# Transposing all 128 rows of every token tile, the last one of an expert included

## The chip, the cores and the metric

The kernel runs on one core of a Trainium2 chip (trn2). The metric is the device time of one execution in microseconds (us). Six terms recur: PE is the matrix engine TensorE, PEld its weight loads (they are shown as a row of their own because they can run beside a matmul), ACT is ScalarE, DVE is VectorE, POOL is GpSimd, and SP issues most of the DMA transfers. PSUM is the memory that PE writes its results to, in banks of 512 float32 columns.

## The reference

Two stages are chained. The first is a gated linear attention over 4 batches, 8 heads, 768 steps and 48 dimensions per head. Its output, laid out as 3072 tokens of 384 numbers, goes through a mixture of 8 experts: every token goes to the one expert with its largest gate logit.

```python
for t in range(S):                                   # attention
    state = f[:, :, t, :, None] * state + np.einsum('bhd,bhe->bhde', k[:, :, t], v[:, :, t])
    y[:, :, t] = np.einsum('bhd,bhde->bhe', q[:, :, t], state)
...
for e in range(E):                                   # experts, x: 3072 x 384
    mask = e_idx == e
    h = np.maximum(x[mask] @ w1[e], 0.0)             # 384 -> 1024
    ye = h @ w2[e]                                   # 1024 -> 384
    out[mask] = gate_w[mask, None] * eom[mask, e, None] * ye
```

## The kernel before, in words

**Two stages.** Up to about 130 us of the span the kernel computes the attention in 24 chunks of 128 tokens, writes every finished token row into a slot of a DRAM table (`xs_dram`) that belongs to its expert, and starts on the first expert. From then on it runs the eight experts one after the other, sorted by their number of tokens, the largest first (`Experts.run`).

**The slots of an expert.** The expert at place s is given a fixed number of token columns, `CAPS = (512, 448, 432, 416, 400, 400, 384, 376)`. Its tokens come from DRAM as tiles of `TS` = 128 rows (`tokens_in`, line 655, always whole tiles of 128 rows; a slot without a token holds a row that was cleared in advance). `rows(s)` (line 641) cuts the capacity into tiles: 448 is 128 + 128 + 128 + 64, so the last tile of that expert counts 64 rows, and those of the following ones 48, 32, 16, 16, 128 (384 is three whole tiles) and 120. The expert at place 0 has four whole tiles.

**One expert.** For each expert PE computes `mm1` (line 750: eight groups of 9 matmuls, 384 to 1024, because each float32 operand is split into a high and a low part and three products are made) and then `mm2` (line 773, or `mm2_rows`, line 787, for experts with at most three tiles: 72 matmuls, 1024 to 384). A matmul of `mm1` or `mm2` streams as many columns as the expert has token columns, 512 down to 376, so it gets shorter from expert to expert. ACT and DVE take each group out of PSUM (lines 765 and 766) and split the weights of the next expert (`split`, line 630).

**The step that the change touches.** `mm1` needs the tokens with the 384 features on the partitions, while they come from DRAM with a token per partition. So `x_in(s, c)` (line 721) turns them, for each of the `KC` = 3 pieces c of 128 features: one PE transpose per tile into columns j*128 of one PSUM tile `x_ps`, then `x_split` (line 714) takes the capacity's columns out: ACT makes the high part `xh` (line 717), DVE the low part `xl` (line 718). A transpose is a weight load of the tile's piece followed by a matmul against the identity. `x_tr` (line 709) passes the tile's count n of rows: the transpose loads n rows, uses an n x n identity and writes n columns. The whole tiles and the short one of an expert follow each other directly, three or four transposes in a row; such a row of transposes is called a block here. There is one `x_ps` tile only (pool `psx`, one buffer), so a block waits until DVE has finished with the block before it.

**What sets the order.** Each engine executes its instructions in the order in which the program is written (`chain`, line 1054, fixes it for DVE, ACT, POOL and PE). In `run`, the three `x_in` blocks of expert s+1 and the weight splits for its `mm1` are spread over the eight steps of `mm2` of expert s: the list `front` (lines 891 to 896) holds them, and one entry is taken out after each step f (or after two of three steps in `mm2_rows`). So 21 blocks stand in the middle of `mm2` matmuls, three per expert from place 1 to 7. The transposes of the expert at place 0 stand elsewhere (`x_early`, `x_late`) and are of whole tiles. The way back, after `mm2`, is `put` (line 811): PE transposes the result tile by tile, ACT scales it, and POOL scatters the rows to the output.

Of the kernel before, what the change touches and what calls it, by code (L numbers as in the profile page):

```python
# [26 lines left out]
TS = 128  # L27
# [100 lines left out]
def attention(ctx, tc, nc, k, kpool, rt, q01, k01, f01, q23, k23, f23, v, wg, xs_dram, r, ex):  # L128
# [334 lines left out]
    for t in range(last + 1):  # L463
# [32 lines left out]
        if hot(t - 2):  # L496
            x_tr(t - 2)
# [52 lines left out]
    scatter(len(sq))  # L550
    evac_y(last)
    x_tr(last - 1)
    run_pq()
    evac_x(last - 1)
    ex.mm1_early(0)
    x_tr(last)
    evac_x(last)
    route(len(RG) - 1, last - 1, 2)
# [19 lines left out]
class Experts:  # L578
# [128 lines left out]
            self.gq.pop(0)()  # L707

    def x_tr(self, s, c, ps, j, col):
        t, n = self.xg[s, j]  # L710
        self.nc.tensor.transpose(out=ps[:, col:col + n], in_=t[0:n, c * 128:(c + 1) * 128],  # L711
                                 identity=self.k.ident[0:n, 0:n])

    def x_split(self, pool, c, ps, n, width, name):
        hi = pool.tile([128, width], F32R, name=f"{name}h{c}")
# [417 lines left out]
```

## Time and profile before

| what | value |
|---|---|
| time, median of 3 runs | 380.4 us (378.98 to 382.08) |
| the profiled execution's own time | 383.17 us |
| its span | 381.4 us |
| mean granted clock of PE | 0.998 of full speed |
| busy in the span: PE, PEld, DVE, ACT, POOL | 95%, 88%, 62%, 52%, 38% |
| DMA: bytes moved, mean rate | 67.75 MB, 178 GB/s |

The span is the time from the first to the last instruction that the profiler saw; the execution's own time has 1.8 us around it. The times of the profile below count from the span's start. A busy PE is not a PE at its peak, because matmuls are pipelined and each is shown from its start to the end of its pipeline; what PE really delivers is read from the distance between the starts of neighbouring matmuls.

### The profile page before, as it was taken

Reading aid. Unit: us, or ns where it says so; the run is one execution under the profiler, and the core shown is the slowest. Engines: PE = TensorE matmul, PEld = TensorE weight load, DVE = VectorE, ACT = ScalarE, POOL = GpSimd, SP = SyncE. Lnnn points to the kernel's source line nnn. Section 1 sums busy time; section 2 is a strip of 40 time slices with the busy share of each in tenths; the row PEclk is TensorE's granted clock in tenths of the full one; section 3 lists DMA queues with packets and bytes.
Section 4 is the critical chain, followed back from the end, with each engine's and each line's share of the span. In section 5 each row is a group of like instructions: output and inputs, shape, how many; then the busy total and the mean of one; then the engine's idle time right before and its main releaser. Section 6 shows DMA issues by size and latency. Waiting matters only on the chain. (4 is left out here: it accounts for less than half of the span.)

```text
span 381.4 us, 8425 instructions
## 1 busy us (share of the span) xinstructions
PE 363.3 (95%) x3199; PEld 334.6 (88%) x3199; DVE 234.7 (62%) x482; ACT 197.7 (52%) x468; POOL 145.8 (38%) x176
## 2 busy tenths in 40 slices
PE   7899999998979999999999999999999999999993
PEld 2688978897868899989989999999999999999993
DVE  6988979897994773655644545463554554554610
ACT  3576856865745641536525634543652653753510
POOL 6686787997968670002201210310220220233012
PEclk9999999999999999999999999999999999999999
DMA  8999999999139327853434353445354354331001
GB/s 262 350 358 358 310 245 247 290 274 281 47 108 306 137 93 235 306 170 123 148 99 171 137 171 128 158 158 169 125 188 147 125 177 157 124 101 42 16 23 41
DMA packets 49315, 67.75 MB, mean 178 GB/s; under 512 B 3682, under 2 KB 43893, under 8 KB 49264
## 3 DMA queue, kind: packets, MB, share of 16 engines
q1 hardware_dynamic: 45952, 57.46, 49.6%
q0 software_dynamic: 3312, 9.65, 7.0%
q8 instruction: 27, 0.44, 0.5%
q14 instruction: 24, 0.20, 0.2%
HBM read 54.16 MB, written 13.39 MB: 177 GB/s over the span
## 5 line engine op out<-in xcount | busy, mean ns | idle before, releaser
L822 POOL DMA_INDIRECT out<-o,dst x30 | 30.2, 1007 | 188.3 <-ACT o L817 102.6
L766 DVE SCALAR_TENSOR_TENSOR hl<-h_ps,hh 128x256 fp32r<-128x256 f32 (+6 forms) x72 | 39.3, 546 | 53.1 <-ACT hh L765 52.3
L761 PE MATMUL h_ps<-xh,w1h 128*128 128x400 f32 (+6 forms) x192 | 67.3, 351 | 0.3 <-DVE hl L766 0.3
L761 PE MATMUL h_ps<-xh,w1l 128*128 128x400 f32 (+6 forms) x192 | 65.0, 338 | 0.0
L761 PE MATMUL h_ps<-xl,w1h 128*128 128x400 f32 (+6 forms) x192 | 64.9, 338 | 0.0
L765 ACT ACTIVATE hh<-h_ps 128x256 fp32r<-128x256 f32 (+6 forms) x72 | 34.8, 484 | 50.3 <-PE h_ps L761 48.6
L783 PE MATMUL y_ps<-hh,w2h 128*128 128x256 f32 (+4 forms) x168 | 57.7, 343 | 0.0
L783 PE MATMUL y_ps<-hl,w2h 128*128 128x256 f32 (+4 forms) x168 | 55.7, 332 | 0.0
L783 PE MATMUL y_ps<-hh,w2l 128*128 128x256 f32 (+4 forms) x168 | 55.6, 331 | 0.0
L718 DVE TENSOR_TENSOR xl<-x_ps,xh 128x400 fp32r<-128x400 f32 (+6 forms) x23 | 13.1, 568 | 41.8 <-ACT xh L717 38.5
L761 PEld LDWEIGHTS h_ps<-xh,w1h 128*128 128x128 f32 x192 | 36.1, 188 | 1.2 <-DVE hl L766 0.5
L761 PEld LDWEIGHTS h_ps<-xl,w1h 128*128 128x128 f32 x192 | 36.2, 188 | 0.4
L761 PEld LDWEIGHTS h_ps<-xh,w1l 128*128 128x128 f32 x192 | 36.0, 188 | 0.5
L717 ACT CAST xh<-x_ps 128x400 fp32r<-128x400 f32 (+6 forms) x23 | 11.3, 490 | 48.5 <-PE x_ps L711 42.4
L224 POOL TENSOR_TENSOR q_t<-q_t,p 128x512 f32<-128x512 f32 x24 | 30.6, 1276 | 9.6 <-DVE p L210 8.0
L637 DVE TENSOR_TENSOR w2l<-w2r,w2h 128x768 fp32r<-128x768 f32 x31 | 30.7, 991 | 4.2 <-ACT w2h L636 1.3
L783 PEld LDWEIGHTS y_ps<-hh,w2h 128*128 128x128 f32 x168 | 31.6, 188 | 1.0
L783 PEld LDWEIGHTS y_ps<-hl,w2h 128*128 128x128 f32 x168 | 31.6, 188 | 0.5
L783 PEld LDWEIGHTS y_ps<-hh,w2l 128*128 128x128 f32 x168 | 31.7, 188 | 0.4
L246 PE MATMUL a_ps<-q_t,k_t 64*128 64x128 f32 x384 | 28.3, 285 | 3.3 <-DVE k_t L221 2.7
L210 DVE TENSOR_TENSOR_SCAN p<-f_ps,start_p 128x511 f32<-128x511 f32 x22 | 28.0, 1273 | 3.9 <-ACT start_p L198 2.2
L323 PE MATMUL x_ps<-turn,xt 128*128 128x112 f32 x192 | 26.2, 280 | 3.8 <-ACT xt L317 3.6
(175 smaller groups left out, 773.1 us busy)
## 6 DMA issues: line engine op xcount, KB each, us to landing
w1r<-in_w SPq DMA_DIRECT2D x32, 384.0 KB
w2r<-in_w SPq DMA_DIRECT2D x32, 384.0 KB
xg<-xs_dram SPq DMA_DIRECT2D x5, 802.0 KB
xs_dram<-empty SPq DMA_DIRECT2D x8, 401.0 KB
f_t<-in_f SPq DMA_DIRECT2D x6, 512.0 KB
q_t<-in_q SPq DMA_DIRECT2D x6, 512.0 KB
k_t<-in_k SPq DMA_DIRECT2D x6, 512.0 KB
v_t<-in_v SPq DMA_DIRECT2D x6, 512.0 KB
```

The costliest lines, as they stand in the source:

```text
L210: nc.vector.tensor_tensor_scan(out=flat(d["p"])[:, 1:n], data0=flat(d["f"])[:, 0:n - 1], data1=sp[:, 1:n], initial=sp[:, 0:1], op0=ALU.mul ...
L224: nc.gpsimd.tensor_tensor(out=q_t[i][:, :, sl], in0=q_t[i][:, :, sl], in1=d["p"], op=ALU.mult)
L246: nc.tensor.matmul(aps[t][par][:, g, :], k_t[b % 2][r, g, sl], q_t[b % 2][r, g, sl], start=(g == 0), stop=(g == NP - 1))
L323: nc.tensor.matmul(xps[t][:, g, :], xt[t][:, g, :], turn[:, g, :], start=(g == 0), stop=(g == NP - 1))
L637: (eng or self.nc.vector).tensor_tensor(out=flat(lo), in0=flat(t), in1=flat(hi.bitcast(F32)), op=ALU.subtract)
L717: self.nc.scalar.copy(out=hi[:, 0:n], in_=ps)
L718: self.nc.vector.tensor_tensor(out=lo[:, 0:n], in0=ps, in1=hi.bitcast(F32)[:, 0:n], op=ALU.subtract)
L761: nc.tensor.matmul(ps[:, 0:n], a[:, c, cs], b, start=(i == 0), stop=(i == 3 * KC - 1))
L765: nc.scalar.activation(out=hi, in_=ps[:, 0:n], func=AF.Relu)
L766: nc.vector.scalar_tensor_tensor(out=lo, in0=ps[:, 0:n], scalar=0.0, in1=hi.bitcast(F32), op0=ALU.max, op1=ALU.subtract)
L783: self.nc.tensor.matmul(self.ys[d][:, c0:c0 + n], a[:, f % 2, ds], b, start=(f == 0 and i == 0 and part == 0), stop=(f == KF - 1 and i == ...
L822: self.nc.gpsimd.indirect_dma_start(out=self.out, out_offset=bass.IndirectOffsetOnAxis(ap=self.k.dst[0:n, j, s:s + 1], axis=0), in_=t[0:n] ...
```

## The change

The transpose of a token tile no longer asks how many rows of the tile count. It loads all 128 rows, uses the whole identity and writes 128 columns. This concerns the last tile of the experts at places 1 to 5 and 7 (64, 48, 32, 16, 16 and 120 rows), three transposes each, so 18 of the 90 transposes at this line. The columns of `x_ps` beyond the expert's capacity are written and not read: `x_split` still takes out the capacity's columns only. All matmuls, evacuations, splits and transfers keep their number, shape and place; the instructions of every engine stand in the same order as before. After the change the lines below this one have a number lower by one.

```diff
     def x_tr(self, s, c, ps, j, col):
-        t, n = self.xg[s, j]
-        self.nc.tensor.transpose(out=ps[:, col:col + n], in_=t[0:n, c * 128:(c + 1) * 128],
-                                 identity=self.k.ident[0:n, 0:n])
+        t, _ = self.xg[s, j]
+        self.nc.tensor.transpose(out=ps[:, col:col + TS], in_=t[:, c * 128:(c + 1) * 128], identity=self.k.ident)
```

## Rows read from the trace of the kernel before

**Rows 1.** Page, part 1: busy us, share of the span, instructions, by engine.
```profile
PE 363.3 (95%) x3199; PEld 334.6 (88%) x3199; DVE 234.7 (62%) x482; ACT 197.7 (52%) x468; POOL 145.8 (38%) x176
```

**Rows 2.** Busy time by stretch: stretch, length, busy of each engine, PE clock, DMA.
```profile
268.00:298.00 30.00, 30.00 (x171) 28.93 (x170) 15.87 (x32) 15.10 (x30) 4.38 (x5) 1.00 0.45 147
```

**Rows 3.** Waits of PE and PEld from 120 us on: us in total, times, longest.
```profile
PE h_ps L761 <- DVE hl L766: 0.7, 2, 0.3
...
PE x_ps L711 <- DVE xl L718: 0.2, 1, 0.2
...
PEld x_ps L711 <- issue: 2.5, 15, 0.2
```

**Rows 4.** Groups by shape, line 711: busy us, mean ns | idle before, releaser.
```profile
L711 PE MATMUL x_ps<-ident,xg 128*128 128x128 f32 x60 | 10.0, 273 | 0.2 <-DVE xl L718 0.2
...
L711 PE MATMUL x_ps<-ident,xg 16*128 16x16 f32 x6 | 1.4, 230 | 0.0
...
L711 PEld LDWEIGHTS x_ps<-ident,xg 16*128 16x128 f32 x6 | 0.8, 133 | 1.0 <-issue 1.0
```

**Rows 5.** Timeline of PE around a block ending in 64 rows: start, length, instruction.
```profile
160.13 0.28 PE L783 MATMUL y_ps<-hl,w2h 128*128 128x256 f32 x1
...
160.84 0.28 PE L783 MATMUL y_ps<-hl,w2h 128*128 128x256 f32 x1
...
161.80 0.28 PE L783 MATMUL y_ps<-hh,w2l 128*128 128x256 f32 x1
```

**Rows 6.** The same around a block ending in 48 rows.
```profile
190.13 0.36 PE L783 MATMUL y_ps<-hh,w2l 128*128 128x448 f32 x1
...
190.93 0.36 PE L783 MATMUL y_ps<-hl,w2h 128*128 128x448 f32 x1
...
192.05 0.37 PE L783 MATMUL y_ps<-hh,w2l 128*128 128x448 f32 x1
```

**Rows 7.** The same around a block ending in 32 rows.
```profile
222.04 0.36 PE L783 MATMUL y_ps<-hh,w2l 128*128 128x432 f32 x1
...
222.81 0.36 PE L783 MATMUL y_ps<-hl,w2h 128*128 128x432 f32 x1
...
223.91 0.36 PE L783 MATMUL y_ps<-hh,w2l 128*128 128x432 f32 x1
```

**Rows 8.** The same around a block ending in 16 rows.
```profile
252.93 0.35 PE L783 MATMUL y_ps<-hl,w2h 128*128 128x416 f32 x1
...
253.49 0.35 PE L783 MATMUL y_ps<-hl,w2h 128*128 128x416 f32 x1
...
254.56 0.35 PE L783 MATMUL y_ps<-hh,w2l 128*128 128x416 f32 x1
```

**Rows 9.** The same around a block of three whole tiles.
```profile
312.38 0.34 PE L783 MATMUL y_ps<-hh,w2l 128*128 128x400 f32 x1
...
313.11 0.34 PE L783 MATMUL y_ps<-hl,w2h 128*128 128x400 f32 x1
...
313.81 0.34 PE L783 MATMUL y_ps<-hh,w2l 128*128 128x400 f32 x1
```

**Rows 10.** The same around the six whole transposes of `x_late`.
```profile
146.55 0.28 PE L783 MATMUL y_ps<-hl,w2h 128*128 128x256 f32 x1
...
147.45 0.28 PE L783 MATMUL y_ps<-hh,w2l 128*128 128x256 f32 x1
```

**Rows 11.** Timeline of ACT, 159 to 168 us.
```profile
161.69 0.54 ACT L717 CAST xh<-x_ps 128x448 fp32r<-128x448 f32 x1 [1.54 <-PE x_ps L711]
...
163.26 0.82 ACT L636 CAST w1h<-w1r 128x768 fp32r<-128x768 f32 x1
```

**Rows 12.** Timeline of DVE, 159 to 168 us.
```profile
162.25 0.62 DVE L718 TENSOR_TENSOR xl<-x_ps,xh 128x448 fp32r<-128x448 f32 x1 [1.02 <-ACT xh L717]
...
164.11 0.96 DVE L637 TENSOR_TENSOR w1l<-w1r,w1h 128x768 fp32r<-128x768 f32 x1 [1.14 <-ACT w1h L636]
...
165.31 0.61 DVE L718 TENSOR_TENSOR xl<-x_ps,xh 128x448 fp32r<-128x448 f32 x1
```

**Rows 13.** Timeline of PE, 165.8 to 167.2 us: the third block of expert 1.
```profile
165.98 0.75 PE L711 MATMUL x_ps<-ident,xg 128*128 128x128 f32 x4 [0.22 <-DVE xl L718]
...
166.88 0.28 PE L783 MATMUL y_ps<-hh,w2l 128*128 128x256 f32 x1
```

## The prediction

> **What bounds the kernel now.** I began with the engines' busy time: PE is busy for 363.3 of 381.4 us, DVE for 62% of the span, the others for less [rows 1]. An average hides stages, so I next read busy time by stretch, which shows where the blocks of transposes stand. The stretch shown covers about one expert of 400 columns: PE is busy for all of its 30.00 us at a granted clock of 1.00 (the 2.4 GHz level), ACT and DVE for about half of it, DMA for 0.45 [rows 2]. The third view is the list of waits. From 120 us on PE has next to none on another engine: 0.7 us in front of `mm1`, and a single 0.2 us in front of a transpose block [rows 3]. So in the expert stage the time is the sum of the distances between PE's starts, and whatever PE no longer spends comes off the end, unless another engine then turns out late.
>
> The same list has the line that this change is about: the weight load of a transpose stood idle 15 times, 2.5 us in all, for "issue", that is for nothing that the profile sees, so 0.17 us each [rows 3]. The groups by shape say which loads: the six that load 16 rows have 1.0 us of it [rows 4]. Of the 18 short transposes 15 load 64, 48, 32 or 16 rows, and three load 120. Fifteen stalls, and no such stall ahead of a whole load, fit one reading: a load that uses a small part of the array's rows does not follow directly on loads that use all of them. I take the stall as tied to that switch, and price it, and whatever it costs on the way back to whole loads, from PE's starts.
>
> **What one block costs.** The measure is the same for every block: the time from the start of the last `mm2` matmul ahead of it to the start of the second one behind it, less two ordinary distances between `mm2` matmuls. (The second one, because the first is shown from before its own weights are in.)
> - 64 rows: 160.84 to 161.80 is 0.96. Ordinary distance: 160.13 to 160.84 holds six, 0.118 each. The block costs 0.72 [rows 5].
> - 48 rows: 190.93 to 192.05 is 1.12; four distances in 0.80, 0.20 each; 0.72 [rows 6].
> - 32 rows: 1.10, four in 0.77, 0.193 each; 0.715 [rows 7].
> - 16 rows: 1.07, three in 0.56, 0.187 each; 0.70 [rows 8].
> - three whole tiles: 0.70, four in 0.73, 0.183 each; 0.335 [rows 9].
> - six whole tiles: 0.90, less twice the 0.118 of rows 5; 0.665 [rows 10].
>
> From three to six whole transposes it is 0.33 us, so one more whole transpose costs 0.11 us; three cost three times that, so whole blocks carry no fixed charge. A block of four whole ones should cost 0.335 + 0.11 = 0.445 us. That is what each block with a short tile becomes.
>
> **The change, edit by edit.** The gains per block are 0.28 (64 rows), 0.275 (48), 0.27 (32) and 0.255 (16); each is larger than the 0.17 us of shown stall because the first whole load behind the short one is late too. The three blocks that end in 120 rows show no stall (they are not among the 15); a whole transpose takes 273 ns from start to end and the shortest, of 16 rows, 230 [rows 4], so going from 120 to 128 rows is worth between nothing and three times the whole 43 ns, 0.13 us; I take nothing, since 120 lies next to 128. The wider columns of the other 15 are inside the 0.11 us of a whole transpose, which I have charged in full. The identity and the rows beyond the count are in place already: tiles come from DRAM whole, so no transfer, evacuation or wait is added.
>
> The rest is where the gain can be lost. Block 3 of expert 1 waits for DVE's `xl` of block 2, because there is one `x_ps` buffer [rows 13]. Two chains end there. PE's own: blocks 1 and 2 become shorter, so PE arrives 0.56 us earlier. DVE's: its `xl` of block 2 starts at 165.31, right behind other work in DVE's queue, which begins with a weight split at 164.11 that waited for ACT's split at 163.26; that in turn follows, through ACT's cast at 161.69 and DVE's `xl` at 162.25, on the end of block 1 [rows 11, 12]. This chain starts from one shortened block and therefore moves by 0.28, not by 0.56. So the wait at block 3 grows from 0.22 to about 0.50 us, and the gain of block 2 is lost there. Block 3 itself starts behind the wait and ends 0.90 us later [rows 13]; with four whole loads I expect about 0.62, the same 0.28 less.
>
> In the other experts the blocks are some 4 us apart (three blocks ahead of each `mm1`, each with 0.5 us of ACT and 0.6 us of DVE behind it [rows 11, 12]) and none of them shows a wait on DVE [rows 3], so I let their gains stand in full. DMA at 0.45 and ACT and DVE at about half [rows 2] have room for an expert that is 0.8 us shorter out of 30.
>
> Sum: expert 1: 0.28 + 0 + 0.28 = 0.56; the expert with 48: 3 x 0.275 = 0.83; with 32: 3 x 0.27 = 0.81; the two with 16: 6 x 0.255 = 1.53. Together 3.7 us. The span goes from 381.4 to 377.7 us and the profiled execution's own time from 383.2 to about 379.5. That execution was 2.8 us slower than the median of the runs; the gain is a fixed number of PE stalls, so I take it off the median: 380.4 - 3.7 = **376.7 us**. Starts are shown to 0.01 us, so a block's price is good to 0.02 and the sum to about 0.3: from 3.4 to 4.0, the 4.0 being the case in which block 2 of expert 1 counts too.
>
> **The rivals.**
> 1. *The stall is not the short load's.* It could belong to the last transpose of a block of four, or to the wider destination, and remain; then the change only adds columns. The place is the same 15 blocks, the price is the longer matmul: between 6 x 43 ns = 0.26 us (only the 16-row ones, priced by the difference of 273 and 230 ns) and 15 x 43 ns = 0.65 us, so about +0.4 and **380.8 us**, slower than before. It decides if a block of four whole transposes still shows an issue stall ahead of its fourth load. Against it: the six transposes of `x_late` contain a fourth whole load and cost 0.11 each [rows 10]. No block of exactly four whole tiles stands in `mm2` in this trace. Chance 0.05.
>    The Trainium skill has a rule that speaks for this rival: its page "TensorE: Matmul & The Clock Gate", Part 3, says that a weight load runs beside matmuls in flight only when it addresses another group of rows, which would make the short load the better hidden one and the change a loss. The trace shows the opposite at this place, the 0.17 us of idle ahead of the short load [rows 3]. The same page's Part 2 prices a matmul by its columns at the full clock; by it the 1416 added columns would be an estimated 0.6 us, near the upper end above.
> 2. *The gain is given back on another engine.* In each expert the `mm1` that follows needs the evacuations and splits which ran beside `mm2`. If ACT or DVE were as close to late in the other experts as in expert 1, one block's gain in three would go there as well: 0.56 + 2/3 x (0.83 + 0.81 + 1.53) = 2.7 us, **377.7 us**. For it: expert 1 does show such a wait. Against it: no other block or `mm1` there waits for DVE [rows 3]. Chance 0.10.
> 3. *Only the shown stall goes.* If the late load behind the short one were a charge of the return from transposes to `mm2`, 15 x 0.17 = 2.5 us would be gained, less the lost block: 2.3 us, **378.1 us**. Against it: blocks of whole tiles carry no fixed charge. Chance 0.05.
>
> That the change does not do what it says I exclude: every short transpose appears in its instruction order as a whole one, and nothing else is moved.
>
> **How the numbers follow.** The forecast has 0.80. Its own gain runs from 3.4 to 4.0 us, and the three runs of before lie from 1.4 us below to 1.7 us above their median. The range reaches from 380.4 - 4.0 - 1.5 = 374.9 to the second and third rival with part of that scatter, 379.2. A change of less than 1%, 3.8 us, is about what a measurement of this kernel can't tell from none, and 3.7 us lies just inside: the forecast splits nearly evenly, 0.41 to 0.38, into within 1% and faster, with 0.01 slower. Rivals 2 and 3 are mostly within 1% (0.12 of 0.15, the rest faster by scatter), rival 1 too (0.04, and 0.01 slower). Together: faster 0.41, within 1% 0.57, slower 0.02.
>
> **What would show it.** In the profile after: no issue wait ahead of the transposes' weight loads; all transposes 128x128; from the last `mm2` matmul before a block to the second behind it about 0.68 us at 256 columns, 0.845 at 448, 0.83 at 432, 0.82 at 416 and 0.81 at 400; the wait of expert 1's third block on DVE up from 0.2 to about 0.5 us; the blocks with 384 and 376 columns unchanged; a span near 377.7. I am wrong if four whole transposes cost more than 0.5 us, or if new waits of PE on DVE or ACT appear in the experts from place 2 on.

## The result and the profile after

The changed kernel takes **376.11 us** (median of 4 runs, 375.80 to 376.77) against 379.87 us before (4 runs, 378.98 to 382.08): ratio **0.9895**, 95% interval 0.9848 to 0.9942, so 3.8 us less. Predicted were 376.7 us and 3.7 us less. Medians and ratios, here and below, leave out the runs that took over 1.5% longer than the fastest of the same kernel (two of the nine of e3, two of the 25 of before that belong to e5 to e8).

First the page and the waits. The page's engine row of the changed kernel answers to [rows 1]:

```profile
PE 359.5 (96%) x3199; PEld 334.9 (90%) x3199; DVE 232.1 (62%) x482; ACT 197.9 (53%) x468; POOL 146.7 (39%) x176
```

The number of instructions is the same. The groups by shape of the transposes (the columns are those of [rows 4]) now have one shape only. Of the 1.8 us that their weight loads stand idle 0.9 go to one wait on DVE, and the rest are gaps of at most 0.06 us:

```profile
L711 PE MATMUL x_ps<-ident,xg 128*128 128x128 f32 x78 | 12.0, 273 | 0.7 <-DVE xl L717 0.7
...
L711 PEld LDWEIGHTS x_ps<-ident,xg 128*128 128x128 f32 x78 | 9.6, 140 | 1.8 <-DVE xl L717 0.9
```

Its waits from 120 us on (us, times, longest) answer to [rows 3]. The 15 issue waits of 2.5 us at line 711 are gone, the wait on DVE at one block has grown from 0.2 to 0.7 us, and the one in front of `mm1` is what it was:

```profile
PE x_ps L711 <- DVE xl L717: 0.7, 1, 0.7
PE h_ps L760 <- DVE hl L765: 0.7, 2, 0.3
...
PEld x_ps L711 <- DVE xl L717: 0.9, 1, 0.9
```

Now what a block costs. This is PE's timeline of the changed kernel (start, length, instruction): for one block each with 64, 48, 32 and 16 counted rows, the last `mm2` matmul ahead of it and the second behind it, as in [rows 5 to 8]; around them the second matmul behind the first expert's six transposes, as in [rows 10], and the last matmul of all.

```profile
143.67 0.28 PE L782 MATMUL y_ps<-hh,w2l 128*128 128x256 f32 x1
...
157.07 0.28 PE L782 MATMUL y_ps<-hl,w2h 128*128 128x256 f32 x1
157.20 0.60 PE L711 MATMUL x_ps<-ident,xg 128*128 128x128 f32 x4
...
157.76 0.28 PE L782 MATMUL y_ps<-hh,w2l 128*128 128x256 f32 x1
...
186.77 0.36 PE L782 MATMUL y_ps<-hl,w2h 128*128 128x448 f32 x1
...
187.61 0.37 PE L782 MATMUL y_ps<-hh,w2l 128*128 128x448 f32 x1
...
217.84 0.36 PE L782 MATMUL y_ps<-hl,w2h 128*128 128x432 f32 x1
...
218.67 0.36 PE L782 MATMUL y_ps<-hh,w2l 128*128 128x432 f32 x1
...
247.75 0.35 PE L782 MATMUL y_ps<-hl,w2h 128*128 128x416 f32 x1
...
248.57 0.35 PE L782 MATMUL y_ps<-hh,w2l 128*128 128x416 f32 x1
...
367.82 0.34 PE L796 MATMUL y_ps<-w2l,hh 128*120 128x384 f32 x1
```

From pair to pair it is 0.69, 0.84, 0.83 and 0.82 us, where it was 0.96, 1.12, 1.10 and 1.07. Less two ordinary distances (0.118, 0.20, 0.193, 0.187) a block costs 0.44 to 0.455 us at every size.

**The span misleads here.** It fell by 7.3 us, from 381.4 to 374.1. The last matmul of the kernel before, in PE's timeline:

```profile
375.04 0.34 PE L797 MATMUL y_ps<-w2l,hh 128*120 128x384 f32 x1
```

From the second matmul behind the first expert's transposes to the last matmul, which from here on is called the expert stage, the kernel before takes 375.04 - 147.45 = 227.59 us [rows 10] and the changed one 367.82 - 143.67 = 224.15. Only **3.44 us** of the 7.3 lie in the stage that the change touches. The other 3.8 lie ahead of it, where no instruction differs. Whether they belong to the change is the first question for the experiments.

### The profile page after: what moved, and what is told of

It is laid out like the page before. It is cut to its first block, busy times and chain, and to the rows that moved or that the text cites. A ratio compares the mean times of both kernels' runs of the same rounds, so it can differ in the third digit from the quotient of the medians.

```text
span 374.1 us, 8425 instructions
## 1 busy us (share of the span) xinstructions
PE 359.5 (96%) x3199; PEld 334.9 (90%) x3199; DVE 232.1 (62%) x482; ACT 197.9 (53%) x468; POOL 146.7 (39%) x176
## 5 line engine op out<-in xcount | busy, mean ns | idle before, releaser
L821 POOL DMA_INDIRECT out<-o,dst x30 | 31.2, 1040 | 183.1 <-ACT o L816 101.7
L246 PEld LDWEIGHTS a_ps<-q_t,k_t 64*128 64x128 f32 x384 | 23.6, 187 | 6.7 <-POOL k_t L221 1.9
```

The source lines that it names most:

```text
L246: nc.tensor.matmul(aps[t][par][:, g, :], k_t[b % 2][r, g, sl], q_t[b % 2][r, g, sl], start=(g == 0), stop=(g == NP - 1))
L821: self.nc.gpsimd.indirect_dma_start(out=self.out, out_offset=bass.IndirectOffsetOnAxis(ap=self.k.dst[0:n, j, s:s + 1], axis=0), in_=t[0:n] ...
```

## The experiments

The expert stage, in us from each run's own profile, is the finer measure; the times of whole runs carry the first stage with them. "First stage until" is the start of that same second matmul.

| kernel | first stage until | last matmul | expert stage | median time | ratio to before (95%) |
|---|---|---|---|---|---|
| before | 147.45 | 375.04 | 227.59 | 379.87 | |
| changed | 143.67 | 367.82 | 224.15 | 376.11 | 0.9895 (0.9848 to 0.9942) |
| e1 before, once more | 145.76 | 373.39 | 227.63 | 381.24 | 1.0029 (0.9999 to 1.0059) |
| e2 at least 64 rows | 144.95 | 373.21 | 228.26 | 380.81 | 1.0017 (0.9997 to 1.0038) |
| e3 at least 65 rows | 144.19 | 368.43 | 224.24 | 377.11 | 0.9937 (0.9905 to 0.9969) |
| e4 changed, two buffers | 144.23 | 367.48 | 223.25 | 375.73 | 0.9888 (0.9864 to 0.9912) |
| e5 before, short one first | 144.89 | 371.86 | 226.97 | 381.15 | 0.9964 (0.9935 to 0.9993) |
| e6 changed, a short one more | 144.32 | 374.53 | 230.21 | 384.97 | 1.0071 (1.0038 to 1.0104) |
| e7 changed, a whole one more | 147.63 | 374.04 | 226.41 | 380.70 | 0.9971 (0.9939 to 1.0002) |
| e8 before, two buffers | 145.15 | 372.34 | 227.19 | 380.32, one run | |

e1 to e4 share one set of runs of before (median 380.28 us), e5 to e8 another (381.87 us).

### e1: the kernel before, once more

No edit.

> The kernel before once more, with a profile of its own. In the two profiles so far the changed kernel's expert stage, from the second matmul behind the six transposes of the first expert to the last matmul, is 224.15 us against 227.59 before (3.44 less), but its attention stage is also 3.8 us shorter, although no instruction there differs. Theory (the change acts in the expert stage alone, the attention stage scatters from execution to execution): the expert stage is 227.6 us again, within 0.1, and the attention stage falls anywhere between 142.9 and 146.7 us. Rival (the change shortens the attention stage too): that stage ends near 146.7 us again. Time ratio to before 1.000.

The expert stage is 227.63 us, 0.04 from the first profile, and the first stage ends at 145.76 us, in the middle between the two. Over the ten profiles it ends anywhere from 143.67 to 147.63 us, the latest in e7, a variant of the changed kernel. The first block that the edit alters starts at 157.20 us in the changed kernel, behind that stage. So the 3.8 us ahead of the expert stage are scatter between executions; what makes the first stage scatter stays open. The same program against itself came out at 1.0029: a ratio of whole runs says little below 0.3%.

### e2 and e3: 64 rows against 65

```diff
         t, n = self.xg[s, j]
+        n = max(n, 64)          # e3: max(n, 65)
         self.nc.tensor.transpose(out=ps[:, col:col + n], in_=t[0:n, c * 128:(c + 1) * 128],
```

> The kernel before, but the short transposes take at least 64 rows and columns (64, 64, 64, 64, 64, 120). Theory (a load of at most 64 rows does not follow directly on loads of all rows, and the way back costs as well): the 15 blocks keep their price, all near the 0.72 us of the block with 64 rows; 15 issue waits of 0.17 us; expert stage 227.6 to 227.9 us, time ratio 1.000. Rival (the price comes from few columns or few rows as such, and falls as the tile is filled up): half of the gain already, ratio 0.995.

> The kernel before, but the short transposes take at least 65 rows and columns (65, 65, 65, 65, 65, 120): one row more than in the run with 64. Theory (64 rows and fewer are loaded in another division of the array, 65 are not): the issue waits are gone, the 15 blocks cost 0.445 us as four whole transposes do, expert stage 224.1 us, ratio 0.990 as with the change. Rival (the stall belongs to the last transpose of a block, or to one that does not fill the tile): as with 64 rows, 15 issue waits, ratio 1.000.

PE's weight loads around one block of an expert with 16 counted rows, with at least 64 rows (e2):

```profile
281.45 0.43 PEld L712 LDWEIGHTS x_ps<-ident,xg 128*128 128x128 f32 x3
282.04 0.14 PEld L712 LDWEIGHTS x_ps<-ident,xg 64*128 64x128 f32 x1 [0.17 <-issue]
282.24 0.19 PEld L784 LDWEIGHTS y_ps<-hh,w2h 128*128 128x128 f32 x1
```

and with at least 65 (e3; the row is labelled by its first load):

```profile
277.53 0.54 PEld L712 LDWEIGHTS x_ps<-ident,xg 128*128 128x128 f32 x4
278.03 0.19 PEld L784 LDWEIGHTS y_ps<-hh,w2h 128*128 128x128 f32 x1
```

Three loads, a gap of 0.17 us, the short load, and the way back: 0.79 us from the first load to the next `mm2` load. With one row and one column more the four loads form one piece and it is 0.50 us. The whole list of waits says the same: in e2

```profile
PEld x_ps L712 <- issue: 2.5, 15, 0.2
```

and in e3 no such line. e3's expert stage is the changed kernel's to 0.1 us. This separates the theories: neither the last place in the block nor a tile that is not full makes the stall, the boundary lies between 64 and 65 rows. (The streamed columns go from 64 to 65 with them; the end of the section on e6 and e7 parts the two.) The Trainium skill, in "TensorEngine Tiling (Array Packing)", Key Properties, says that a change of the array's division into tiles drains the engine, and the same page lists, under Available Configurations, divisions of 128, of 64 and of 32 rows; the trace agrees, with 0.17 us ahead of the load of 64 rows and none ahead of the one of 65. e2 went 0.4 us beyond what I expected: a block with 64 rows costs 0.725 to 0.745 us in the experts that have 16 rows before, where it is 0.675 to 0.695. e3's ratio, 0.9937, is worse than its stage alone would make it (3.35 us less, 0.991), though its interval reaches down to 0.9905. Its runs scatter more than the changed kernel's (375.94 to 379.76 us), and only one of them has a profile, so in which stage the others lose time is not shown.

### e5: the short tile first

```diff
-        for j, _ in self.rows(s):
+        for j, _ in reversed(self.rows(s)):
             self.x_tr(s, c, ps, j, j * TS)
```

> The kernel before, but the tiles of a block are transposed in reverse order, the short one first. Theory (the price is that of a load of at most 64 rows between loads of all rows, wherever it stands): the 15 blocks keep their price of 0.70 to 0.72 us, the issue wait stands ahead of the short load again; since ACT now gets its input only behind the whole price, the third block of expert 1 waits some 0.2 us longer; expert stage 227.6 to 227.9 us, ratio 1.000. Rival (the stall belongs to the last of four transposes): it moves to a whole load, and the block no longer waits ahead of the short one.

Weight loads of the kernel before with reversed blocks, one block of the expert with 48 rows:

```profile
188.14 0.19 PEld L783 LDWEIGHTS y_ps<-hl,w2h 128*128 128x128 f32 x1
188.62 0.50 PEld L711 LDWEIGHTS x_ps<-ident,xg 48*128 48x128 f32 x4 [0.30 <-issue]
```

The gap stays with the short load, as the theory has it, and is longer, 0.30 us: that load now follows a matmul of 448 columns rather than one of 128. Twelve of the 15 are listed (3.3 us in all); in expert 1, behind matmuls of 256 columns, two gaps are 0.13 us, too short for the list, and the third load waits for DVE. But the expected stage was missed by 0.6 us: the blocks cost 0.645 to 0.685 us instead of 0.70 to 0.72. So the whole price is about 0.04 us smaller, on average over the 15 blocks, where the short load stands between an `mm2` matmul and a whole transpose than where it stands the other way round; which of its two switches is the cheaper one there, the runs do not show. The wait of expert 1's third block did grow by 0.2 us (to 0.4). Position matters for a sixth of the price, not for its existence.

### e6 and e7: a short or a whole transpose more per block

```diff
+        self.nc.tensor.transpose(out=ps[:, 0:16], in_=self.xg[s, 0][0][0:16, c * 128:(c + 1) * 128],
+                                 identity=self.k.ident[0:16, 0:16])      # e7: self.x_tr(s, c, ps, 0, 0)
         for j, _ in self.rows(s):
             self.x_tr(s, c, ps, j, j * TS)
```

> The changed kernel with one more transpose at the start of each of the 21 blocks, of 16 rows, whose result the next transpose overwrites. Theory: each block pays the switch (0.25 us) and a transpose (0.11 us), 0.36 us; expert 1's wait gives back one of three, so 7.2 us: expert stage 224.15 + 7.2 = 231.4 us, ratio to before about 1.009; 21 issue waits. Rival (a short transpose costs no more than a whole one where it is not the last of four): 2.2 us, expert stage 226.4 us, ratio 0.995.

> The counterpart of the run before it: the changed kernel with one more transpose of all 128 rows at the start of each of the 21 blocks, overwritten by the next. Theory: a whole transpose costs 0.11 us, and four in a row as much as four times one, so 2.2 us: expert stage 226.4 us, ratio about 0.995; no issue wait. Rival (a block of more transposes has a fixed charge of its own): as much as with the short one, 231 us.

Weight loads of one block of the expert with 448 columns, with the short one added (e6):

```profile
187.75 0.19 PEld L784 LDWEIGHTS y_ps<-hl,w2h 128*128 128x128 f32 x1
188.24 0.13 PEld L722 LDWEIGHTS x_ps<-ident,xg 16*128 16x128 f32 x1 [0.30 <-issue]
188.40 0.42 PEld L711 LDWEIGHTS x_ps<-ident,xg 128*128 128x128 f32 x4
188.79 0.19 PEld L784 LDWEIGHTS y_ps<-hh,w2h 128*128 128x128 f32 x1
```

and with the whole one added (e7):

```profile
190.79 0.19 PEld L783 LDWEIGHTS y_ps<-hl,w2h 128*128 128x128 f32 x1
190.99 0.67 PEld L711 LDWEIGHTS x_ps<-ident,xg 128*128 128x128 f32 x5
191.63 0.19 PEld L783 LDWEIGHTS y_ps<-hh,w2h 128*128 128x128 f32 x1
```

The first whole load starts 0.20 us after the `mm2` load ahead of it, and the five are 0.13 us apart on average; the short one starts 0.49 us after. Over 21 blocks the whole one costs 226.41 - 224.15 = 2.26 us, as expected, 0.11 each; the short one, which loads an eighth of the rows and streams an eighth of the columns, 6.06 us. Expected were 7.2: its block price is 0.30, not 0.36 (e6 pays the cheaper position, as e5). 18 of the 21 show the issue wait, 4.9 us in all. Of the three of expert 1, where `mm2` matmuls have 256 columns, two wait 0.13 to 0.14 us, too short for the list, and cost 0.31 as well; the third waits for DVE.

PE's timeline beside these loads shows what the short load waits for. In e6:

```profile
187.95 0.36 PE L784 MATMUL y_ps<-hl,w2h 128*128 128x448 f32 x1
188.24 0.23 PE L722 MATMUL x_ps<-ident,xg 16*128 16x16 f32 x1
```

and in e7:

```profile
190.99 0.36 PE L783 MATMUL y_ps<-hl,w2h 128*128 128x448 f32 x1
```

The whole load of e7, at 190.99, starts together with the matmul ahead of it. The short load of e6, at 188.24, starts 0.07 us before the shown end of the matmul ahead of it (187.95 + 0.36), and the whole load behind it, at 188.40, starts 0.07 us before the shown end of the short transpose. So a load waits at both switches until the matmul ahead is all but through. (Ends of matmuls are modelled in the profile, so the 0.07 us is a mark and not a time on the chip.) In before, e1, e2 and e8 the same 0.07 us stands at all 15 switches to a short load and at all 15 back.

The first stage of the kernel before shows that the switch waits and not every short load. This is one group of its matmuls, with PE first and the weight loads below it:

```profile
114.76 1.16 PE L246 MATMUL a_ps<-q_t,k_t 64*128 64x128 f32 x16
```

```profile
114.76 0.97 PEld L246 LDWEIGHTS a_ps<-q_t,k_t 64*128 64x128 f32 x16
115.85 0.42 PEld L263 LDWEIGHTS kn_ps<-ident,k_t 128*128 128x128 f32 x4
```

Sixteen loads of 64 rows, on the two halves of the rows in turn, follow each other in 0.97 us, about 0.06 us apart. The load of all rows behind them starts, once more, 0.07 us before the shown end of the last matmul (114.76 + 1.16). These matmuls stream 128 columns, so it is the rows that matter, which e2 and e3 alone can't say. A transpose that is short in the columns of its weights and uses all rows costs nothing extra. In PE's timeline of before, three whole transposes of `put` and three with 64 columns of weights stand in `mm1`:

```profile
209.95 0.36 PE L761 MATMUL h_ps<-xh,w1l 128*128 128x432 f32 x1
...
210.67 0.35 PE L761 MATMUL h_ps<-xl,w1h 128*128 128x432 f32 x1
...
212.03 0.35 PE L761 MATMUL h_ps<-xh,w1l 128*128 128x432 f32 x1
212.22 0.49 PE L814 MATMUL o_ps<-ident,y 128*64 128x128 f32 x3
...
212.75 0.36 PE L761 MATMUL h_ps<-xl,w1h 128*128 128x432 f32 x1
```

Both pairs are 0.72 us apart.

### e4 and e8: a second buffer

```diff
         self.psy, self.pso = pool("mo_psy", 1, space=PSUM), pool("mo_pso", 1, space=PSUM)
+        self.psx2 = pool("mo_psx2", 1, space=PSUM)
...
-        ps = self.psx.tile([128, 512], F32, name="x_ps")
+        ps = (self.psx2 if c == 1 else self.psx).tile([128, 512], F32, name="x_ps")
```

> The changed kernel with a second x_ps buffer in PSUM for the middle piece of features, so that the third block of expert 1 no longer waits for DVE to empty the second one's. Theory (in the changed kernel that wait, 0.7 us, swallows the gain of two of expert 1's blocks): the wait is gone, the expert stage falls from 224.15 to about 223.4 us, ratio to before 0.988. Rival (the wait comes back a little later, at the first mm1 matmuls of expert 1, because ACT and DVE are as late as before): expert stage 224.1 us, ratio 0.990.

> The kernel before with the second x_ps buffer. Theory: only the wait of 0.2 us at the third block of expert 1 goes, expert stage 227.3 us; with the second buffer on both sides the change is then worth 227.3 - 223.25 = 4.05 us, the sum of all 15 blocks' gains (3.95 by the prediction's prices), while with one buffer 0.6 us of it went into DVE's wait. Rival (the buffer shifts something else): a stage that differs from 227.3 by more than 0.2 us.

Expert 1's third block in PE's timeline, in the changed kernel with one buffer:

```profile
161.13 0.28 PE L782 MATMUL y_ps<-hl,w2h 128*128 128x256 f32 x1
162.13 0.66 PE L711 MATMUL x_ps<-ident,xg 128*128 128x128 f32 x4 [0.73 <-DVE xl L717]
162.54 0.36 PE L782 MATMUL y_ps<-hh,w2h 128*128 128x256 f32 x1
162.75 0.28 PE L782 MATMUL y_ps<-hh,w2l 128*128 128x256 f32 x1
```

and with two (e4):

```profile
161.71 0.29 PE L783 MATMUL y_ps<-hl,w2h 128*128 128x256 f32 x1
161.84 0.60 PE L712 MATMUL x_ps<-ident,xg 128*128 128x128 f32 x4
162.19 0.37 PE L783 MATMUL y_ps<-hh,w2h 128*128 128x256 f32 x1
162.40 0.28 PE L783 MATMUL y_ps<-hh,w2l 128*128 128x256 f32 x1
```

From the last matmul ahead of the block to the second behind it, 1.62 us become 0.69, the price of any other block there, and the wait does not return in `mm1`, where PE waits for DVE 0.7 us in all with one buffer and with two: the stage falls by 0.90 us to 223.25. In the kernel before, the second buffer is worth 0.40 us. So with two buffers on both sides the change brings 227.19 - 223.25 = **3.94 us**, and with one buffer 3.44: the 0.5 us between them are what DVE's wait took. e4 is the best version of the study by its profile; its time (ratio 0.9888) can't be told from the changed kernel's.

## Why the prediction was right, step by step

- **The bound.** PE's own sequence sets the expert stage: what its blocks lost came off the end. The sum of the 15 blocks, from PE's starts in both profiles, is 3.40 us; the stage lost 3.44.
- **The stall as the price of switching.** Right, and shown by e3 against e2, by e6 against e7, and by the missing issue line after. That the price is the switch's and not the short load's own is read from the first stage, where loads of 64 rows follow each other without it. That 120 rows cost nothing extra fits: their blocks take 0.68 us in both profiles.
- **Four whole transposes at 0.445 us.** Measured 0.44 to 0.455 at all four sizes.
- **Gains per block.** The expert with 48 rows: predicted 0.83, measured 3.38 - 2.53 = 0.85 (three blocks, pair to pair). With 32: 0.81, measured 3.28 - 2.50 = 0.78. The two with 16: 1.53, measured 6.33 - 4.89 = 1.44.
- **Block 2 of expert 1 is lost to DVE.** Right in kind: e4 and e8 give 0.5 us back to the change when the buffer is doubled.
- **The time.** 3.7 us were predicted from the trace, 3.44 are in the stage, 3.76 between the medians. The difference of the last two lies inside the scatter of the first stage, so it is luck that the medians come out within 0.1 us of the 3.7: the stage itself gained 0.3 us less than the sum, 0.23 of it in expert 1. The ratio's interval reaches from 0.6% to 1.5%, so it does not decide whether the change is above or below 1%, over which I had split the chances.

**Expert 1.** The mechanism was right and its size was not: the term of 0.56 us measured 3.32 - 2.99 = 0.33. I let the chain to DVE's second `xl` move by the whole 0.28 us that block 1 gains. ACT's cast starts when the last transpose of the block is done, and it moved less. Before, in PE's timeline, the block starts at

```profile
160.96 0.69 PE L711 MATMUL x_ps<-ident,xg 128*128 128x128 f32 x4
```

and ACT at 161.69 [rows 11], 0.73 us later. After, the block starts at 157.20 (in the first timeline above). ACT's timeline goes on with

```profile
157.83 0.53 ACT L716 CAST xh<-x_ps 128x448 fp32r<-128x448 f32 x1 [1.44 <-PE x_ps L711]
...
159.41 0.82 ACT L636 CAST w1h<-w1r 128x768 fp32r<-128x768 f32 x1
```

and DVE's with

```profile
158.40 0.62 DVE L717 TENSOR_TENSOR xl<-x_ps,xh 128x448 fp32r<-128x448 f32 x1 [0.93 <-ACT xh L716]
...
160.26 0.96 DVE L637 TENSOR_TENSOR w1l<-w1r,w1h 128x768 fp32r<-128x768 f32 x1 [1.14 <-ACT w1h L636]
...
161.46 0.61 DVE L717 TENSOR_TENSOR xl<-x_ps,xh 128x448 fp32r<-128x448 f32 x1
```

That is 0.63 us after the block's start. Only 0.10 us of the 0.28 lay ahead of the last transpose's result; the rest lies behind it, on the way back to whole loads, where PE pays and ACT does not wait. The chain behind it moved by the same 0.1: from ACT's cast to DVE's second `xl` it is 3.63 us after and 3.62 before [rows 11, 12]. So PE's wait grew to 0.73 us and not to 0.50. Block 3 itself became 0.28 us shorter behind the wait (162.13 to 162.75, 0.62 against the 0.90 of [rows 13]), as predicted.

**The rivals.** The stall stays and only columns are added: excluded by e3, and by the four whole transposes of the profile after. The gain given back in every expert: only expert 1 shows a wait. Only the shown stall goes: the stage lost 3.44 us, not 2.3. The Trainium skill's sentence in "TensorE: Matmul & The Clock Gate", Part 3, that I had put beside the first rival, by which a load overlaps only with matmuls on another group of rows, does not describe this case. The short loads, whose rows are some of those of the matmul ahead, are the ones that wait, 0.30 us in e5; and a load of all rows does start beside a running matmul on all rows: in e7 the load at 190.79 (above) begins with this matmul of PE's timeline:

```profile
190.79 0.36 PE L783 MATMUL y_ps<-hh,w2l 128*128 128x448 f32 x1
```

## What to carry to other kernels

A transpose that uses 64 rows or fewer, set between transposes and matmuls that use all rows, cost 0.24 to 0.28 us more here than a whole one, although it does less; where the padding rows exist anyway, use them. Price such a thing by the starts of the neighbours on the engine that sets the time, not by the shown duration or the shown stall, which was 0.17 of the 0.28. And where a shorter block feeds a chain on other engines, ask which part of the gain lies ahead of its last result: only that part reaches the chain.

## What the runs showed of the hardware that was not expected

- Both switches wait, the one to a short load and the one back: each load starts 0.07 us before the shown end of the matmul ahead, while loads of the same rows start beside it (e6, e7). Among themselves loads of 64 rows run about 0.06 us apart (first stage of before).
- The price hardly falls with the rows: 0.675 to 0.695 us per block with 16 rows and 0.725 to 0.745 with 64 (e2), but 0.445 with 65 (e3).
- The short load at the start of a block waits 0.30 us, at its end 0.17, and yet the block is 0.04 to 0.05 us cheaper with it at the start (e5).
- The first stage, of identical instructions, ended between 143.67 and 147.63 us in ten profiles, which is as much as the whole effect of the change; the expert stage repeated to 0.04 us (e1).
